# An MLP behind a spectral mixer: its products cut to 256 columns, the three terms summed in the same PSUM columns, Mish read from PSUM

## The chip, the core and the metric

The kernel runs on one core of one Trainium2 chip. The metric is the device time of one execution in microseconds, lower is better. A core has TensorE (PE; its weight loads are shown as PEld), VectorE (DVE), ScalarE (ACT), GpSimd (POOL) and SyncE (SP), each with its own instruction queue worked off in order, a scratch memory of 128 partitions (SBUF) and the accumulators that TensorE writes (PSUM, eight banks of 512 fp32 columns in each partition).

## The reference

For x of 2048 rows by 512, fp32:

```
mod = (silu(c) @ w_mod) -> sa, ca, ga, sb, cb, gb
h = layernorm(x) * (1 + ca) + sa
x = x + ga * irfft2(rfft2(h) * (w_r + i w_i))
h = layernorm(x) * (1 + cb) + sb
x = x + gb * (mish(h @ w1 + b1) @ w2)        # w1: 512 x 1376, w2: 1376 x 512
```

## The kernel before, in words

The first 130 us are the Fourier part, as products with constant matrices. Its end (`p3_col`, `p3_row`) runs over 16 groups of 128 rows; then comes the MLP, which the change touches.

**Precision.** Each MLP operand is split into a high part (a rounded fp32r copy, made by ScalarE) and a low part (the rest, made by VectorE). A product is three terms, high x high, high x low, low x high (`TERMS`); low x low is left out.

**Tiling.** The rows go in 8 blocks (`NB`) of 256 (two groups of 128). The 1376 hidden columns are 10 tiles of 128 and a narrow one of 96. A block has 6 steps (`NT`): step 0 has the narrow tile alone, steps 1 to 5 have two tiles each. In the last block step 0 comes last (`item`).

**First product, `up`.** For a tile of hidden columns the weights w1 (128 x 128 pieces, four along the 512 inputs) are the stationary operand, and the block's input h streams, its high and low part side by side as 2 x 256 columns. Four products with w1's high part stream all 512 columns into a bank: high x high in its columns 0 to 255, high x low in 256 to 511. Four with w1's low part stream the 256 high columns into 0 to 255. So the result lies in two halves that are still to be added.

**Activation, `front` and `back`.** Per tile ScalarE reads the right half of the bank and adds the bias b1 (L813), VectorE adds the left half (L814); then one Mish on ScalarE over both tiles, 512 columns in SBUF (L820), and four small sums and differences on VectorE (L830).

**Second product, `halves` and `down`.** `halves` splits the activations (`ah`, `al`, L765 and L766). `down` is done two steps after `up` (`LAG`). For a pair of hidden tiles and two groups of rows it uses a scheme with seven instead of eight block products (`RAW`, `SUM`, `END`), each 256 columns and three terms: 21 products a step (L856). Step 0 instead has 2 x 3 products of 512 columns with 96 rows of weights (L848). The last block does steps 3, 4, 5 and 0 in the plain way with 512 columns (`last_down`, L868 and L871).

**Next block's input.** In step 3 ScalarE normalises the next block's rows (`norm_pair`), in step 4 TensorE transposes them (`transpose_in`, L693, eight fp32 transposes), and ScalarE and VectorE scale, shift and split them (`split_in`, L701, L705, L706).

**Order.** The MLP is written out by hand: `mlp(s, parts)` gives each engine's queue its order. In step 4 TensorE has `up`, the transposes, then `down` of two steps ago. PSUM banks go by four tags A to D, two banks each, in rotation: A and D alternate for the two tiles of a step and serve the transposes; C, B, B, C are the four outputs of a block. The tile framework sets the waits between engines.

Of the kernel before, what the change touches and what calls it, by code (L numbers as in the profile page):

```python
# [9 lines left out]
AF = mybir.ActivationFunctionType  # L10
ALU = mybir.AluOpType

P = 128
S, D, F = 2048, 512, 1376
# [8 lines left out]
TERMS = ((0, 0), (0, 1), (1, 0))  # L23
# [3 lines left out]
LAG = 2  # L27
# [4 lines left out]
def tile_spectral_block(ctx: ExitStack, tc: tile.TileContext, x_d, w1_d, b1_d, w2_d,  # L32
                        c_d, xt_d, wm_d, wq_d, wz_d, kr_d, km_d, kc_d, ki_d, kf_d, kv_d, kw_d, kp_d, out_d):
    nc = tc.nc
# [33 lines left out]
    def bank(tag):  # L68
        return psum.tile([P, 512], F32, name="bank", tag=tag)

    def buf(tag, dt=F32):
        return work.tile([P, 512], dt, name="buf", tag=tag)

    def plain(t):
        return t.bitcast(F32)
# [6 lines left out]
    b1n = base.tile([P, NF], F32, name="b1n")  # L82
# [75 lines left out]
    def norm(n, late=False):  # L158
        h = buf("h")
        if late:  # L160
            nc.scalar.activation(h, x[:, n, :], AF.Identity, scale=rstd[:, n:n + 1], bias=nmr[:, n:n + 1])
            return h
        nc.gpsimd.tensor_scalar(h, x[:, n, :], rstd[:, n:n + 1], nmr[:, n:n + 1],
                                op0=ALU.mult, op1=ALU.add)
        return h

    st = {}
# [418 lines left out]
    with tc.manual_schedule():  # L586
# [13 lines left out]
        for p in range(pairs):  # L600
# [34 lines left out]
            if p in (3, 5):  # L635
                i = p // 2 - 1
# [9 lines left out]
    w1h = pm.tile([P, 4, NF * P], F32R, name="w1h")  # L646
    w1l = pm.tile([P, 4, NF * P], F32R, name="w1l")
    pm.tile([P, 16], F32, name="line")
    w2 = {}
# [24 lines left out]
    def h2_tiles(b):  # L674
        if b % 2 == 0:
            h2[b] = pm.tile([P, 4, 2, 256], F32R, name="h2e", tag="h2e")
        else:
            h2[b] = big.tile([P, 4, 2, 256], F32R, name="h2o", tag="cr")
# [4 lines left out]
    def norm_pair(n):  # L683
        st["h2", n] = norm(n, True), norm(n + 1, True)

    def transpose_in(n, g):
        if g == 0:
            h2_tiles(n // 2)
        st["pt2", g] = ps = bank("AD"[g] if n else "D")
        hs = st["h2", n]  # L690
        for k in range(2):
            for i, h in enumerate(hs):
                nc.tensor.transpose(ps[:, (2 * k + i) * P:(2 * k + i + 1) * P],  # L693
                                    h[:, (2 * g + k) * P:(2 * g + k + 1) * P], ident)

    def split_in(n, g):
        ps = st.pop(("pt2", g))
        t = buf("t")
        for e in reversed(range(2)):
            k = 2 * g + e  # L700
            nc.scalar.activation(t[:, 256 * e:256 * e + 256], ps[:, 256 * e:256 * e + 256],  # L701
                                 AF.Identity, bias=cols[:, 1, 0, k:k + 1], scale=cols[:, 1, 1, k:k + 1])
        tv = t.rearrange("p (k s) -> p k s", k=2)
        hh, hl = (h2[n // 2][:, 2 * g:2 * g + 2, i, :] for i in range(2))
        nc.scalar.copy(hh, tv)  # L705
        nc.vector.tensor_tensor(hl, tv, plain(hh), op=ALU.subtract)  # L706
# [36 lines left out]
    def item(g):  # L743
        b, i = divmod(g, NT)
        return b, (i + 1) % NT if b == NB - 1 else i

    def tiles(t):
        return [(0, NF - 1, F - (NF - 1) * P)] if t == 0 else [(e, 2 * t - 2 + e, P) for e in range(2)]
# [43 lines left out]
    ups, acts, out_ps, done = {}, {}, {}, {}  # L792
    tsum = modr[:, 0:2].rearrange("p r (e d) -> p (r e) d", d=256)

    def up(g):
        b, t = item(g)
        h = h2[b]
        ups[g] = []
        for e, f, rows in tiles(t):
            ps = bank("CD"[e] if g < 2 else "AD"[e])[:rows]  # L800
            fs = slice(f * P, f * P + rows)
            for k in range(4):
                nc.tensor.matmul(ps, w1h[:, k, fs], h[:, k], start=(k == 0), stop=False)  # L803
            for k in range(4):
                nc.tensor.matmul(ps[:, 0:256], w1l[:, k, fs], h[:, k, 0], start=False, stop=(k == 3))  # L805
            ups[g].append((e, f, ps))

    def front(g):
        st["w", g] = w = buf("g1")
        for e, f, ps in ups.pop(g):  # L810
            rows = ps.shape[0]
            o = w[:rows, 256 * e:256 * e + 256]
            nc.scalar.activation(o, ps[:, 256:], AF.Identity, bias=b1n[:rows, f:f + 1])  # L813
            nc.vector.tensor_tensor(o, o, ps[:, 0:256], op=ALU.add)  # L814

    def back(g):
        b, t = item(g)
        w = st.pop(("w", g))
        o = w if t else w[:96, 0:256]
        nc.scalar.activation(o, o, AF.Mish)  # L820
        if t == 0:
            return [(o, slice(0, 2))]
        if b == NB - 1 and t > 2:
            return [(w, slice(0, 4))]
        u = buf("g2")
        a = w.rearrange("p (e s) -> p e s", s=P)
        v = u.rearrange("p (e s) -> p e s", s=P)
        for o, p, q, op in ((v[:, 0], a[:, 0], a[:, 2], ALU.add), (v[:, 1], v[:, 0], a[:, 1], ALU.subtract),
                            (v[:, 2], a[:, 1], a[:, 0], ALU.subtract), (v[:, 3], a[:, 3], v[:, 1], ALU.subtract)):
            nc.vector.tensor_tensor(o, p, q, op=op)  # L830
        return [(w[:, P:], slice(0, 3)), (u, slice(3, 7))]

    def halves(g, parts):
        hi, lo = acts[g] = [act.tile([P, 7, P], F32R, name=n) for n in ("ah", "al")]
        for r, c in parts:
            split(*(z[:r.shape[0], c].rearrange("p e s -> p (e s)") for z in (hi, lo)), r)

    def down(g):
        b, t = item(g)
        if b == NB - 1 and t not in (1, 2):  # L840
            return last_down(g, t)
        a = acts.pop(g)
        out = out_ps.setdefault(b, None) or [bank(n) for n in "CBBC"]
        out_ps[b] = out
        if t == 0:
            for n, half in ((1, 1), (2, 0)):
                for i, (p, q) in enumerate(TERMS):
                    nc.tensor.matmul(out[n], a[p][:96, half], w2[0][q][:96], start=(i == 0), stop=False)  # L848
            return
        last = b == NB - 1  # L850
        end = t == (2 if last else 5)
        for n, half, e, r in END if last and end else RAW + SUM:
            o = out[n][:, 256 * half:256 * half + 256]
            own = last or n in (0, 3)
            for i, (p, q) in enumerate(TERMS):
                nc.tensor.matmul(o, a[p][:, e], w2[t][q][:, r], start=(own and half == 0 and t == 1 and i == 0),  # L856
                                 stop=(end and i == 2 and (n, half) != (1, 0)), skip_group_check=own)

    def last_down(g, t):
        a = acts.pop(g)  # L860
        if t == 3:
            out_ps["last"] = bank("A"), bank("D")
        for half in range(2):
            o = out_ps["last"][half]
            for f in range(2 if t else 1):
                for i, (p, q) in enumerate(TERMS):
                    if t:
                        nc.tensor.matmul(o, a[p][:, half + 2 * f], w2["plain", t][q][:, 512 * f:512 * f + 512],  # L868
                                         start=(t == 3 and f == 0 and i == 0), stop=False)
                    else:  # L870
                        nc.tensor.matmul(o, a[p][:96, half], w2[0][q][:96], start=False, stop=(i == 2))  # L871

    rows = modr[:, 0:2]

    def gather(b):
        out = out_ps[b]
        p, q = buf("h"), buf("h")
        nc.scalar.copy(p, out[0])
        nc.scalar.copy(q, out[3])
        done[b] = p, q  # L880
# [28 lines left out]
    def mlp(s, parts):  # L909
        b, i = divmod(s, NT)  # L910
        nxt = 2 * b + 2 if b < NB - 1 else None
        up(s)
        if i == 4 and nxt:
            for g in range(2):
                transpose_in(nxt, g)
        front(s)
        halves(s - 1, parts)
        parts = back(s)
        if i == 3 and nxt:
            norm_pair(nxt)  # L920
        if i == 4 and nxt:
            for g in range(2):
                split_in(nxt, g)
        down(s - LAG)
        if i == 1 and b:
            gather(b - 1)
            chain(b - 1)
        if i == 2 and b:
            residual(b - 1)
        if s == total - 3:  # L930
            gather(b)
            chain(b)
        if s == total - 2:
            residual(b)
        return parts
# [54 lines left out]
    h, l = (w.rearrange("p e d -> p (e d)")[:, 768:] for w in w2[3])  # L990
    nc.vector.tensor_tensor(l, tsum.rearrange("p e d -> p (e d)"), plain(h), op=ALU.subtract)
    halves(0, back(0))
    parts = back(1)
    load_w2(4)
    sum_w2(4, 0, 1, 2, 3)
# [164 lines left out]
```

## Time and profile before

| what | value |
|---|---|
| median of 3 runs | 379.59 us (379.28 to 380.18) |
| profiled execution | 379.18 us |
| its span, first to last instruction | 377.4 us |
| granted TensorE clock | 0.998 of full |
| busy: TensorE, weight loads, VectorE, ScalarE, GpSimd | 371.6, 332.9, 292.3, 240.0, 91.4 us |
| products and weight loads | 2809 each |
| the MLP's stretch | from 133.7 us to the end |

The page's busy time of TensorE is the union of overlapping products, so it says that one follows the other, not how fast they go. Rows of the chain of waits give a start, a length and a line with the count of instructions; rows of the timeline give start, length, engine, line, operation, output and inputs. In names, h2e and h2o are the inputs of even and odd blocks, w1h and w1l the parts of w1, w, w2hi, w2a, w2b, w2c the places of w2's parts, ah and al the activations' parts.

### The profile page before, as it was taken

Reading aid. Unit: us, or ns where it says so; the run is one execution under the profiler, and the core shown is the slowest. Engines: PE = TensorE matmul, PEld = TensorE weight load, DVE = VectorE, ACT = ScalarE, POOL = GpSimd, SP = SyncE. Lnnn points to the kernel's source line nnn. Section 1 sums busy time; section 2 is a strip of 40 time slices with the busy share of each in tenths; the row PEclk is TensorE's granted clock in tenths of the full one; section 3 lists DMA queues with packets and bytes.
Section 4 is the critical chain, followed back from the end, with each engine's and each line's share of the span. In section 5 each row is a group of like instructions: output and inputs, shape, how many; then the busy total and the mean of one; then the engine's idle time right before and its main releaser. Section 6 shows DMA issues by size and latency. Waiting matters only on the chain.

```text
span 377.4 us, 7443 instructions
## 1 busy us (share of the span) xinstructions
PE 371.6 (98%) x2809; PEld 332.9 (88%) x2809; DVE 292.3 (77%) x673; ACT 240.0 (64%) x535; POOL 91.4 (24%) x110
## 2 busy tenths in 40 slices
PE   8999999999999999999999999999999999999995
PEld 8899866668999988998999999998998999999984
DVE  1898989892878979879749758857966975988993
ACT  1688856855668447964945845855765674675650
POOL 0587725861974303300000000000000100026000
PEclk9999999999999999999999999999999999999999
DMA  7999998464332211000100100100100200221011
GB/s 241 376 337 344 326 378 320 141 197 131 104 103 73 81 30 56 2 0 8 50 2 1 57 0 2 56 2 1 58 2 0 76 2 0 85 75 67 3 56 56
DMA packets 20164, 36.78 MB, mean 97 GB/s; under 512 B 3713, under 2 KB 6625, under 8 KB 19873
## 3 DMA queue, kind: packets, MB, share of 16 engines
q1 hardware_dynamic: 20128, 36.31, 28.1%
q8 instruction: 22, 0.36, 0.4%
q14 instruction: 14, 0.11, 0.1%
HBM read 32.10 MB, written 4.20 MB: 96 GB/s over the span
## 4 chain that ended last, share of the span: by engine, by line
PE 94%; DVE 2%; ACT 2%; issue 1%; ACTq 0%
PE bank L856 24%; PE bank L803 21%; PE bank L805 10%; PE bank L531 4%; PE bank L504 4%; PE bank L724 4%; PE bank L715 4%; PE bank L714 4%; PE bank L211 3%; PE bank L256 3%; PE bank L848 3%; PE bank L868 2%; PE bank L693 2%; PE bank L267 1%; PE bank L479 1%; PE bank L257 1%
## 5 line engine op out<-in xcount | busy, mean ns | idle before, releaser
L813 ACT ACTIVATE buf<-bank,b1n 128x256 f32<-128x256 f32 (+1 forms) x88 | 40.8, 472 | 62.7 <-PE bank L805 59.9
L814 DVE TENSOR_TENSOR buf<-buf,bank 128x256 f32<-128x256 f32 (+1 forms) x88 | 35.3, 416 | 35.1 <-ACT buf L813 34.4
L766 DVE TENSOR_TENSOR al<-buf,ah 128x512 fp32r<-128x512 f32 (+2 forms) x85 | 53.7, 656 | 0.7 <-ACT ah L765 0.7
L803 PE MATMUL bank<-h2e,w1h 128*128 128x512 f32 (+1 forms) x176 | 47.9, 394 | 0.0
L803 PE MATMUL bank<-h2o,w1h 128*128 128x512 f32 (+1 forms) x176 | 47.8, 393 | 0.0
L785 POOL TENSOR_TENSOR buf<-buf,modr 128x512 f32<-128x512 f32 (+1 forms) x3 | 3.9, 1299 | 179.2 <-DVE buf L814 172.1
L765 ACT CAST ah<-buf 128x512 fp32r<-128x512 f32 (+2 forms) x85 | 43.0, 548 | 1.2 <-DVE buf L830 1.1
L830 DVE TENSOR_TENSOR buf<-buf 128x128 f32<-128x128 f32 x148 | 39.8, 310 | 3.5 <-ACT buf L820 2.2
L820 ACT ACTIVATE buf<-buf 128x512 f32<-128x512 f32 (+1 forms) x48 | 28.6, 597 | 15.9 <-DVE buf L814 15.8
L856 PE MATMUL bank<-w2a,ah 128*128 128x256 f32 x161 | 34.4, 283 | 0.0
L803 PEld LDWEIGHTS bank<-h2o,w1h 128*128 128x128 f32 (+1 forms) x176 | 29.8, 185 | 4.7 <-DVE buf L814 0.4
L803 PEld LDWEIGHTS bank<-h2e,w1h 128*128 128x128 f32 (+1 forms) x176 | 29.9, 186 | 4.3
L856 PE MATMUL bank<-w2b,ah 128*128 128x256 f32 x147 | 30.6, 277 | 0.0
L805 PEld LDWEIGHTS bank<-h2e,w1l 128*128 128x128 f32 (+1 forms) x176 | 26.5, 185 | 3.9
L805 PEld LDWEIGHTS bank<-h2o,w1l 128*128 128x128 f32 (+1 forms) x176 | 26.5, 185 | 3.9
L805 PE MATMUL bank<-h2e,w1l 128*128 128x256 f32 (+1 forms) x176 | 27.5, 278 | 0.0
L805 PE MATMUL bank<-h2o,w1l 128*128 128x256 f32 (+1 forms) x176 | 27.5, 278 | 0.0
L856 PEld LDWEIGHTS bank<-w2a,ah 128*128 128x128 f32 x161 | 26.3, 188 | 0.0
L715 PE MATMUL bank<-kc,d 128*128 128x128 f32 x128 | 24.8, 275 | 0.0
L714 PE MATMUL bank<-kc,d 128*128 128x128 f32 x128 | 24.7, 275 | 0.0
L856 PEld LDWEIGHTS bank<-w2b,ah 128*128 128x128 f32 x147 | 24.0, 188 | 0.0
L127 DVE BATCH_NORM_STATS2 st<-x 128x6 f32<-128x512 f32 x32 | 22.1, 689 | 0.6
(232 smaller groups left out, 944.8 us busy)
## 6 DMA issues: line engine op xcount, KB each, us to landing
buf<-in_B_w_dram SPq DMA_DIRECT2D x20, 256.0 KB, 2.6
x<-in_A_x_dram SPq DMA_DIRECT2D x16, 256.0 KB, 4.9
xring<-in_x_t_dram SPq DMA_DIRECT2D x16, 256.0 KB, 4.8
out_dram<-x SPq DMA_DIRECT2D x7, 512.0 KB, 2.6
mraw<-in_km_dram SPq DMA_DIRECT2D x16, 128.0 KB, 4.5
wqa<-in_w_q_dram SPq DMA_DIRECT2D x4, 512.0 KB, 6.0
early<-in_w_mod_dram SPq DMA_DIRECT2D x8, 256.0 KB, 6.5
wqb<-in_w_q_dram SPq DMA_DIRECT2D x4, 512.0 KB, 7.2
```

What stands on the lines that cost most here:

```text
L127: nc.vector.bn_stats(t, x[:, n, :])
L714: nc.tensor.matmul(o, dj[:, 0:128], kc[0][:, n, :], start=True, stop=False)
L715: nc.tensor.matmul(o, dj[:, 64:192], kc[1][:, n, :], start=False, stop=True)
L765: nc.scalar.copy(h, r)
L766: nc.vector.tensor_tensor(l, r, plain(h), op=ALU.subtract)
L803: nc.tensor.matmul(ps, w1h[:, k, fs], h[:, k], start=(k == 0), stop=False)
L805: nc.tensor.matmul(ps[:, 0:256], w1l[:, k, fs], h[:, k, 0], start=False, stop=(k == 3))
L813: nc.scalar.activation(o, ps[:, 256:], AF.Identity, bias=b1n[:rows, f:f + 1])
L814: nc.vector.tensor_tensor(o, o, ps[:, 0:256], op=ALU.add)
L820: nc.scalar.activation(o, o, AF.Mish)
L830: nc.vector.tensor_tensor(o, p, q, op=op)
L856: nc.tensor.matmul(o, a[p][:, e], w2[t][q][:, r], start=(own and half == 0 and t == 1 and i == 0), stop=(end and i == 2 and (n, half) != ( ...
```

## The change

All products of the MLP stream 256 columns. In `up` a tile's twelve products (four pieces of the inputs, three terms each) accumulate in the same 256 columns, the two tiles of a step in the two halves of one bank (tag A; C and D for the first two steps). `front` is then one Mish per tile, read from PSUM with the bias, and `back` keeps the four sums and differences. The 512-column products of step 0's `down` and of `last_down` become two of 256. In step 4 the transposes stand behind `down`, both in banks of tag D, as are the last block's two plain outputs. Where several groups share a bank, only its first product clears it.

```diff
 def transpose_in(n, g):
-        st["pt2", g] = ps = bank("AD"[g] if n else "D")
+        st["pt2", g] = ps = bank("D")
 def up(g):
+        ps = bank("CD"[g] if g < 2 else "A")
         for e, f, rows in tiles(t):
-            ps = bank("CD"[e] if g < 2 else "AD"[e])[:rows]
+            o = ps[:rows, 256 * e:256 * e + 256]
             fs = slice(f * P, f * P + rows)
             for k in range(4):
-                nc.tensor.matmul(ps, w1h[:, k, fs], h[:, k], start=(k == 0), stop=False)
-            for k in range(4):
-                nc.tensor.matmul(ps[:, 0:256], w1l[:, k, fs], h[:, k, 0], start=False, stop=(k == 3))
-            ups[g].append((e, f, ps))
+                for i, (p, q) in enumerate(TERMS):
+                    nc.tensor.matmul(o, (w1h, w1l)[p][:, k, fs], h[:, k, q], start=(e == 0 and k == 0 and i == 0),
+                                     stop=(e == len(tiles(t)) - 1 and k == 3 and i == 2), skip_group_check=True)
+            ups[g].append((e, f, o))
 def front(g):
-        for e, f, ps in ups.pop(g):
-            rows = ps.shape[0]
-            o = w[:rows, 256 * e:256 * e + 256]
-            nc.scalar.activation(o, ps[:, 256:], AF.Identity, bias=b1n[:rows, f:f + 1])
-            nc.vector.tensor_tensor(o, o, ps[:, 0:256], op=ALU.add)
+        for e, f, o in ups.pop(g):
+            rows = o.shape[0]
+            nc.scalar.activation(w[:rows, 256 * e:256 * e + 256], o, AF.Mish, bias=b1n[:rows, f:f + 1])
 def back(g):
-        o = w if t else w[:96, 0:256]
-        nc.scalar.activation(o, o, AF.Mish)
 def down(g):
         if t == 0:
             for n, half in ((1, 1), (2, 0)):
                 for i, (p, q) in enumerate(TERMS):
-                    nc.tensor.matmul(out[n], a[p][:96, half], w2[0][q][:96], start=(i == 0), stop=False)
+                    for c in range(0, D, 256):
+                        nc.tensor.matmul(out[n][:, c:c + 256], a[p][:96, half], w2[0][q][:96, c:c + 256],
+                                         start=(i == 0 and c == 0), stop=False, skip_group_check=True)
 def last_down(g, t):
-            out_ps["last"] = bank("A"), bank("D")
+            out_ps["last"] = bank("D"), bank("D")
...
+                    for c in range(0, D, 256):
...
 def mlp(s, parts):
         up(s)
-        if i == 4 and nxt:
-            for g in range(2):
-                transpose_in(nxt, g)
         front(s)
         halves(s - 1, parts)
         parts = back(s)
         if i == 3 and nxt:
             norm_pair(nxt)
+        down(s - LAG)
         if i == 4 and nxt:
             for g in range(2):
+                transpose_in(nxt, g)
+            for g in range(2):
                 split_in(nxt, g)
-        down(s - LAG)
```

**TensorE, step 4 of a block.** The end of `up`, the transposes and the start of `down`; before:

```order
L803 MATMUL bank<-h2e,w1h 128x512 x4
L805 MATMUL bank<-h2e,w1l 128x256 x4
L693 MATMUL bank<-ident,buf 128x128 x8
L856 MATMUL bank<-w2a,ah 128x256 x2
L856 MATMUL bank<-w2a,al 128x256
```

and now:

```order
L805 MATMUL bank<-h2e,w1h 128x256 x2
L805 MATMUL bank<-h2e,w1l 128x256
L855 MATMUL bank<-w2a,ah 128x256 x2
L855 MATMUL bank<-w2a,al 128x256
L693 MATMUL bank<-ident,buf 128x128 x8
L805 MATMUL bank<-h2e,w1h 128x256 x2
```

The second product of two steps ago now stands ahead of the transposes, and the next step's first product directly behind them; within a tile the weights alternate high, high, low.

**ScalarE, start of the MLP** (L131 and L132 are the last group's normalisation, the next rows the first two steps' activations), as a difference:

```order
 L132 ACTIVATE bank<-bank 128x4 [waits Activation_49]
+L813 ACT_TABLE_LOAD
 L813 ACTIVATE buf<-bank,b1n 96x256 [waits PE_49]
-L813 ACTIVATE buf<-bank,b1n 128x256 [waits PE_49] x2
-L820 ACT_TABLE_LOAD
-L820 ACTIVATE buf<-buf 96x256 [waits DVE_49]
+L813 ACTIVATE buf<-bank,b1n 128x256 [waits PE_49]
+L813 ACTIVATE buf<-bank,b1n 128x256
 L765 CAST ah<-buf 96x256 [waits Activation_49]
```

The table of functions is loaded ahead of the first tile, the wait on VectorE's sum is gone, and the two tiles of a step have one wait on TensorE in place of two.

More of the change, by code (lines that the diff above doesn't have):

```diff
@@ L818, in back @@
         w = st.pop(("w", g))
-        o = w if t else w[:96, 0:256]
-        nc.scalar.activation(o, o, AF.Mish)
         if t == 0:
-            return [(o, slice(0, 2))]
+            return [(w[:96, 0:256], slice(0, 2))]
         if b == NB - 1 and t > 2:
@@ L856, in down @@
                 nc.tensor.matmul(o, a[p][:, e], w2[t][q][:, r], start=(own and half == 0 and t == 1 and i == 0),
-                                 stop=(end and i == 2 and (n, half) != (1, 0)), skip_group_check=own)
+                                 stop=(end and i == 2 and (n, half) != (1, 0)), skip_group_check=True)
     def last_down(g, t):
@@ L866, in last_down @@
                 for i, (p, q) in enumerate(TERMS):
[L867 to L871, printed above, removed]
+                    for c in range(0, D, 256):
+                        if t:
+                            l, r = a[p][:, half + 2 * f], w2["plain", t][q][:, 512 * f + c:512 * f + c + 256]
+                        else:
+                            l, r = a[p][:96, half], w2[0][q][:96, c:c + 256]
+                        nc.tensor.matmul(o[:, c:c + 256], l, r, start=(t == 3 and f == 0 and i == 0 and c == 0),
+                                         stop=(t == 0 and i == 2 and c > 0), skip_group_check=True)
     rows = modr[:, 0:2]
```

## The prediction

> **What bounds the kernel now.** I read the page's engine shares first.
>
> ```profile
> PE 371.6 (98%) x2809; PEld 332.9 (88%) x2809; DVE 292.3 (77%) x673; ACT 240.0 (64%) x535; POOL 91.4 (24%) x110
> ```
>
> TensorE sets the end. A busy PE may still be waiting inside a group, so the second view is the chain of waits over one block of six steps, merged by line. Column two is the time from a group's start to the next group's start.
>
> ```profile
> 211.11 0.87 PE bank L693 x8
> 211.98 2.47 PE bank L856 x21
> ...
> 219.71 0.92 PE bank L803 x4
> 220.64 0.47 PE bank L805 x4
> 221.10 2.38 PE bank L856 x21
> 223.48 0.91 PE bank L803 x4
> 224.40 0.47 PE bank L805 x4
> 224.87 0.93 PE bank L803 x4
> 225.80 0.45 PE bank L805 x4
> 226.25 2.38 PE bank L856 x21
> ...
> 230.94 0.45 PE bank L805 x4
> 231.40 1.39 PE bank L848 x6
> ...
> 240.80 0.87 PE bank L693 x8
> ...
> 330.75 2.48 PE bank L856 x21
> ```
>
> One group follows another without a hole, from the transposes at 211.11 to the next at 240.80. So the time is the number of products times their pitch. There are two pitches for the same product of 256 columns: 2.47/21 = 117.6 ns and 2.38/21 = 113.3 ns, held over all 21. Four products of 512 take 0.91 or 0.93, 230 ns each on average, which is two of 115. **Fast stretches** stand only after the narrow tile (the 96 hidden columns, 219.71) and after a tile whose four short products took 0.45. **Slow stretches** follow the transposes, at 211.98 as behind the seventh and last (330.75). Between, the four 512-column products of a tile turn the pitch over: the tile at 223.48 comes out of a fast stretch and ends slow (0.47), the next ends fast again (0.45).
>
> The third view, what the weight loads waited for from 134 us on, has four rows in all, these the longest:
>
> ```profile
> PEld bank L848 <- DVE al L766: 0.5, 1, 0.5
> PEld bank L803 <- DVE buf L814: 0.4, 1, 0.4
> ```
>
> One is where the MLP starts, the other in its last 13 us. The steady part has no wait to remove.
>
> **The change, part by part.**
>
> *Work taken from ScalarE and VectorE.* Per full step two Identity reads of PSUM, two adds and one Mish become two Mish reads of PSUM.
>
> ```profile
> L813 ACT ACTIVATE buf<-bank,b1n 128x256 f32<-128x256 f32 (+1 forms) x88 | 40.8, 472 | 62.7 <-PE bank L805 59.9
> L814 DVE TENSOR_TENSOR buf<-buf,bank 128x256 f32<-128x256 f32 (+1 forms) x88 | 35.3, 416 | 35.1 <-ACT buf L813 34.4
> L820 ACT ACTIVATE buf<-buf 128x512 f32<-128x512 f32 (+1 forms) x48 | 28.6, 597 | 15.9 <-DVE buf L814 15.8
> ```
>
> A Mish from PSUM isn't in the trace; I price it as the Identity of that form, 472 ns (Mish over 512 columns at 597 and two Identities at 472 bound it from 0.3 to 0.6 us). VectorE loses 35.3 us, ScalarE 28.6 us, and all of it lies beside TensorE: worth 0 in the steady part. The first Mish now waits for both tiles of its step, 1.4 us later than the first Identity; its products are used two steps on, so that costs 0.
>
> *The stalls go.* At the start the chain runs through ScalarE:
>
> ```profile
> 138.26 1.22 ACT L813 ACTIVATE buf<-bank,b1n 96x256 f32<-96x256 f32 x3
> 139.50 1.28 ACT L820 ACT_TABLE_LOAD   x1
> 141.24 0.41 ACT L765 CAST ah<-buf 96x256 fp32r<-96x256 f32 x1
> 141.68 0.78 DVE L766 TENSOR_TENSOR al<-buf,ah 96x256 fp32r<-96x256 f32 x1 [0.36 <-ACT ah L765]
> 141.70 0.50 PE L848 MATMUL bank<-w2b,ah 96*128 96x512 f32 x1
> 364.98 1.15 PE bank L803 x4
> 366.60 5.65 PE bank L868 x24
> ```
>
> The first L848 lost 0.5 there to the low half (the wait above). With the table load first, then three Mish (1.22), the cast starts at 138.3 + 1.28 + 1.22 = 140.8 and the low half is ready at 141.6 to 142.0; it is first read four short products after 141.6, at 142.07. I take 0.5 as saved, and 0.2 as the low end. At the end 1.15 against 0.93 is 0.22, and 5.65/24 = 235 against 230 is 0.11: VectorE's adds that made those two late are gone. Sum: **-0.8 us**.
>
> *512 columns become twice 256.* 88 tiles gain 4 products each, the halves of step 0 gain 42, the last block's products 42: 436 more products and weight loads, same columns. In units of 256 the MLP has 88 x 12 + 37 x 21 + 84 + 84 = 2001. Now: the block from 211.98 to 240.80 is 28.82 us for 249 units, 115.8 each, 231.7 us for all. After, no 512 is left to turn the pitch, and every unit is at 113.3 or at 117.6: 226.7 us or 235.3 us, -5.0 or +3.6. Those are the two ends; which units run at which pitch decides. My reading: the transposes set slow, the narrow tile sets fast, all else keeps what it finds. Then slow are: step 0 to the first transposes, 162 units; behind each of the first six transposes 24 + 21 and half a narrow tile, 51, so 306; behind the seventh 279, as no narrow tile comes before the end. Total 747 at 117.6 and 1254 at 113.3: 229.9 us, **-1.8 us**.
>
> [...]
>
> *The fifth step's transposes behind its second product.* The eight transposes (0.87, the change of operand type included) are as many as before, and no DMA moves. They now stand behind the 21 products of L856, before the next step's tiles. On ScalarE everything behind the read of the transposes queues:
>
> ```profile
> 241.21 1.02 ACT L765 CAST ah<-buf 128x384 fp32r<-128x384 f32 x2
> 242.67 1.01 ACT L701 ACTIVATE buf<-bank,cols 128x256 f32<-128x256 f32 x2
> 245.28 0.62 ACT L705 CAST h2e<-buf 128x512 fp32r<-128x512 f32 x1
> 245.94 0.69 DVE L706 TENSOR_TENSOR h2e<-buf,h2e 128x512 fp32r<-128x512 f32 x1 [0.88 <-ACT h2e L705]
> 243.99 1.08 PE L803 MATMUL bank<-h2o,w1h 128*128 128x512 f32 x4
> 246.77 0.28 PE L856 MATMUL bank<-w2hi,ah 128*128 128x256 f32 x1
> 249.24 1.09 PE L803 MATMUL bank<-h2e,w1h 128*96 128x512 f32 x4
> 250.63 0.39 PE L856 MATMUL bank<-w2b,ah 128*128 128x256 f32 x2
> ```
>
> Both reads and casts took 242.67 to 245.90, 3.2 us. In these times they would now start near 244.1 and end at 247.4; VectorE's low half (0.69) makes the new block's input ready near 248.1, needed at 249.24. The next step's Mish (0.9), ready to run at 246.9, is held to 247.4, its casts (1.0) and the last subtraction end near 249.9, needed at 250.63. Margins 1.1 and 0.7 us; 57 products between them at the fast pitch take 0.25 away. I cost the part at 0; if ScalarE's queue ran 1.2 us later than worked out here, TensorE would wait 0.5 us a block, 7 x 0.5 = +3.5 us.
>
> **The sum**: -0.8 - 1.8 + 0 = -2.6. The profiled execution took 379.18 us (span 377.4 and 1.8 around it), the median of three is 379.59, 0.1% more; from the median, **377.0 us**.
>
> **The rivals.**
>
> *A: fast nearly throughout, 373.8 us* (-5.0 - 0.8). The fast stretches last as long as nothing disturbs them, at exactly one pitch, so a slow stream may fall into it by itself. Against: no slow stretch of 21 did. Chance 0.18.
>
> *B: nothing sets fast; slower, 382.4 us* (+3.6 - 0.8). One mechanism: the transposes put TensorE on 117.6, and only the 512s had taken it off. It decides at the narrow tile of each block. For: the very last narrow tile, entered after a wait, took 0.47 for its four short products, no sign of fast. Against: in six blocks 2.38 follows directly on it. Chance 0.22.
>
> ```profile
> 366.12 0.47 PE bank L805 x4
> ```
>
> *C: no change that can be told, 378.8 to 380.0 us.* The change of 128 to 96 rows in L848 sets slow too: its six 512s (231.40) take 232 each although the tile ahead ended fast (230.94). Then only 96 units in each of six blocks are fast, 1425 x 117.6 + 576 x 113.3 = 232.8, +1.1, and with -0.8 the end is at 379.9. So does a fixed price of 2 ns on each extra product, within what the rows allow (2 x 113.3 - 230 = -3, 2 x 117.6 - 230 = +5): 436 x 2 = +0.9, 379.7. With the pitches mixed as now the end is 378.8. [...] Chance 0.20.
>
> **How the numbers follow.** Forecast 0.40, A 0.18, C 0.20, B 0.22. What a measurement can tell from no change is 0.2%, 0.8 us. The forecast and A are faster, and a quarter of C: 0.63. Three quarters of C, less a little that reaches beyond: 0.13. B and that rest: 0.24. The forecast's own range is 375.4 to 378.4 (fast stretches longer or shorter by 250 units, 1.1 us, and the stalls' 0.4). The range to record reaches past A, over C and into the near side of B, where some stretches are fast: 373.5 to 381.9; what lies above is the fully slow half of B and a late split, about 0.15.
>
> **What would show it.** In the chain of waits: x21 groups at 2.38 behind each narrow tile and on to the next transposes, at 2.47 behind the transposes only; a tile of 24 at 2.72 or 2.82, nothing between. B: 2.47 everywhere. C: 2.47 behind L846 (the halves). The waits above should be gone; a wait of TensorE on the new block's input or on a high half, once a block, would show the moved transposes too late. VectorE's busy time should fall to about 257 us and ScalarE's to about 211 with no effect of their own. The prediction is wrong if the pitch changes inside a group, or if a third pitch appears.

## The result, and the profile after

The changed kernel takes 376.96 us (median, 376.28 to 377.35) against 379.43 us before: a ratio on record of 0.9924, 95% interval 0.9907 to 0.9941 (the two medians alone give 0.9935). In a later series it took 377.75 us against 379.94, 0.9938 (0.9920 to 0.9957). It is faster by 0.6 to 0.8%, and the predicted 377.0 us lies between. Much of the spread between the profiled executions lies ahead of the MLP: its first product starts anywhere from 133.5 to 135.7 us, behind stages that no kernel here touches. The sharper measure is therefore the MLP's own stretch, from the start of its first product to the start of the last add in the chain of waits: 239.06 us before, 236.43 us after.

The page of the changed kernel, engine shares and the two groups whose work changed:

```profile
PE 368.0 (98%) x3245; PEld 349.6 (93%) x3245; DVE 261.6 (70%) x585; ACT 213.9 (57%) x487; POOL 91.3 (24%) x110
...
L813 ACT ACTIVATE buf<-bank,b1n 128x256 f32<-128x256 f32 (+1 forms) x88 | 37.3, 471 | 90.8 <-PE bank L805 76.7
L827 DVE TENSOR_TENSOR buf<-buf 128x128 f32<-128x128 f32 x148 | 42.5, 328 | 1.3
```

TensorE is still at 98%. Mish from PSUM takes 471 ns. VectorE and ScalarE have lost 30.7 and 26.1 us of work, which was on the path only at the start of the MLP (see the transposes at their old place, below). L827, the four sums that stood at L830, became slower, 310 to 328 ns each.

The chain of waits of the changed kernel (start, length, group), at the MLP's start, over a block's boundary, and at its end:

```profile
133.46 1.37 PE bank L805 x12
...
135.72 5.66 PE bank L805 x48
...
153.40 0.87 PE bank L693 x8
154.27 2.83 PE bank L805 x24
...
159.57 1.37 PE bank L805 x12
160.94 2.38 PE bank L855 x21
163.32 2.72 PE bank L805 x24
...
229.78 1.37 PE bank L846 x12
231.15 2.73 PE bank L805 x24
...
333.02 2.47 PE bank L855 x21
...
369.89 1.37 DVE x L944 x2
```

There is no third pitch. A tile of 24 takes 2.83 or 2.72 us (118 or 113 ns a product), a group of 21 2.47 or 2.38. Behind the transposes (153.40) both are slow, the narrow tile (159.57) turns the pitch, and from there on all is fast to the next transposes, through step 0's twelve products at 229.78 as well. The last block, with no narrow tile until its end, is slow. Inside a group the pitch changes only in the narrow tile, as the sum had it. The view of waits lists none of TensorE or of its weight loads in the MLP any more; in the kernel before it lists four.

A slow stretch and the fast one behind it, as windows (start and end, length, busy time of TensorE, weight loads, VectorE, ScalarE and GpSimd, then the granted clock, the DMA engines' busy share and GB/s):

```profile
153.40:159.60 6.20, 6.20 (x55) 6.20 (x54) 4.76 (x10) 5.65 (x12) 1.43 (x2) 1.00 0.00 0
159.60:182.70 23.10, 23.10 (x206) 23.10 (x205) 15.94 (x37) 11.47 (x24) 0.00 (x0) 1.00 0.06 24
```

The granted clock is 1.00 in both, and the DMA engines are idle in the slow one, so neither the clock nor transfers make the difference.

### The profile page after: what moved, and what is told of

The parts are those of the page before. It is cut to its first block, busy times and chain, and to the rows that moved or that the text cites. A ratio compares the mean times of both kernels' runs of the same rounds, so it can differ in the third digit from the quotient of the medians.

```text
span 374.3 us, 8202 instructions
## 1 busy us (share of the span) xinstructions
PE 368.0 (98%) x3245; PEld 349.6 (93%) x3245; DVE 261.6 (70%) x585; ACT 213.9 (57%) x487; POOL 91.3 (24%) x110
## 4 chain that ended last, share of the span: by engine, by line
PE 94%; DVE 2%; DMA 1%; ACT 1%; issue 1%; SPq 0%; ACTq 0%
PE bank L805 32%; PE bank L855 24%; PE bank L531 4%; PE bank L504 4%; PE bank L715 4%; PE bank L714 4%; PE bank L724 4%; PE bank L211 3%; PE bank L256 3%; PE bank L846 3%; PE bank L871 2%; PE bank L693 2%; PE bank L479 1%; DMA wmc<-in_w_mod_dram 1%; PE bank L257 1%; PE bank L258 1%
## 5 line engine op out<-in xcount | busy, mean ns | idle before, releaser
L805 PE MATMUL bank<-h2e,w1h 128*128 128x256 f32 (+1 forms) x352 | 62.3, 279 | 0.0
L805 PE MATMUL bank<-h2o,w1h 128*128 128x256 f32 (+1 forms) x352 | 62.1, 278 | 0.0
L805 PEld LDWEIGHTS bank<-h2e,w1h 128*128 128x128 f32 (+1 forms) x352 | 52.8, 185 | 0.0
L805 PEld LDWEIGHTS bank<-h2o,w1h 128*128 128x128 f32 (+1 forms) x352 | 52.8, 185 | 0.0
L805 PE MATMUL bank<-h2e,w1l 128*128 128x256 f32 (+1 forms) x176 | 48.8, 277 | 0.0
L805 PE MATMUL bank<-h2o,w1l 128*128 128x256 f32 (+1 forms) x176 | 48.8, 277 | 0.0
L827 DVE TENSOR_TENSOR buf<-buf 128x128 f32<-128x128 f32 x148 | 42.5, 328 | 1.3
L805 PEld LDWEIGHTS bank<-h2e,w1l 128*128 128x128 f32 (+1 forms) x176 | 32.6, 185 | 0.0
L805 PEld LDWEIGHTS bank<-h2o,w1l 128*128 128x128 f32 (+1 forms) x176 | 32.6, 185 | 0.0
L855 PEld LDWEIGHTS bank<-w2a,ah 128*128 128x128 f32 x161 | 26.1, 188 | 0.0
L701 ACT ACTIVATE buf<-bank,cols 128x256 f32<-128x256 f32 x32 | 16.3, 560 | 8.9 <-PE bank L693 8.9
L256 PE MATMUL bank<-buf,mring 128*128 128x512 f32 x48 | 20.7, 430 | 0.3 <-DVE buf L249 0.2
```

The source lines that it names most:

```text
L256: nc.tensor.matmul(pa, m[:, a, 0:128], g, start=(i == 0), stop=False)
L805: nc.tensor.matmul(o, (w1h, w1l)[p][:, k, fs], h[:, k, q], start=(e == 0 and k == 0 and i == 0), stop=(e == len(tiles(t)) - 1 and k == 3 a ...
```

## The experiments

The table has the profiled execution's MLP stretch, worked out from two rows of the chain of waits as above, and the products counted at each pitch by their starts in the trace (fast up to 115 ns, slow 116 to 119; 23 to 38 products of each kernel take longer, most of them 120 to 123 ns, and are in neither). Where an expectation gives the MLP's length "to its last product", it is 0.6 us more than the stretch given here.

| kernel | stretch, us | slow | fast | time, us | ratio to before (interval) |
|---|---|---|---|---|---|
| before | 239.06 | 512s mixed in | | | |
| changed | 236.43 | 694 | 1280 | 376.96 | 0.9924 (0.9907 to 0.9941) |
| changed, again | 236.52 | 704 | 1264 | 377.75 | 0.9938 (0.9920 to 0.9957) |
| the cut alone | 237.46 | 820 | 1152 | 378.69 | 0.9960 (0.9946 to 0.9975) |
| changed, step 0's six left at 512 | 239.04 | 1216 | 664 | 379.67 | 0.9995 (0.9980 to 1.0010) |
| changed, transposes at the old place | 236.98 | 825 | 1152 | 377.80 | 0.9954 (0.9939 to 0.9970) |
| input early | 235.93 | 494 | 1470 | 377.62 | 0.9947 (0.9928 to 0.9966) |
| narrow tile later at the start | 236.00 | 557 | 1415 | 376.66 | 0.9920 (0.9899 to 0.9941) |
| both | 235.34 | 361 | 1601 | 377.09 | 0.9923 (0.9906 to 0.9940) |
| both, two waits removed | 233.61 | 65 | 1905 | 374.59 | 0.9851 (0.9826 to 0.9876) |

**The cut alone.** The kernel before, with its 512-column products as two of 256 each; halves of the bank, VectorE's add, Mish and the transposes stay.

```diff
-                nc.tensor.matmul(ps, w1h[:, k, fs], h[:, k], start=(k == 0), stop=False)
+                for q in range(2):
+                    nc.tensor.matmul(ps[:, 256 * q:256 * q + 256], w1h[:, k, fs], h[:, k, q],
+                                     start=(k == 0 and q == 0), stop=False, skip_group_check=True)
...
```

> The kernel before with nothing but its 512-column products cut into pairs of 256 (left and right half of the bank, VectorE's add, the separate Mish and the place of the transposes stay). Theory (the pitch of a product is a state that transposes set slow, the narrow tile sets fast, and 512-column products turn over): 1.1 to 1.4 us faster than before, near 378.2, with slow stretches of 21 + 24 + 21 units behind each transposes, fast ones from the third product of each narrow tile, and the waits at the MLP's start and end still there. Rival 1 (the gain came from the work taken off ScalarE and VectorE): no change, 379.4. Rival 2 (a 512-column product is simply dearer than two of 256, the same everywhere): the full steady gain, 2 to 2.5 us, near 377.

The stretch fell by 1.60 us, the time by 1.4. The cut alone brings more than half of the gain, and most of that by the pitch, as its chain of waits shows:

```profile
143.51 0.65 PE bank L852 x4
...
154.41 2.48 PE bank L861 x21
...
162.19 0.92 PE bank L804 x8
...
163.56 2.38 PE bank L861 x21
```

The group behind the transposes is slow, the one behind the narrow tile (162.19) fast. At 143.51 four products take 0.65 us where 0.47 would do: the start's stall is still there. By the products' starts it costs 0.48 us beyond the pitch, where it cost 0.58 before. The waits in the last 13 us, which I expected to stay, are gone, though VectorE's adds are not: TensorE, slow through the whole last block, comes to the narrow tile when they are done (365.4 against 365.3 us). They had cost 0.36 us. So 0.46 of the 1.60 us are waits, and 1.14 are pitch, the low end of what I expected.

**Step 0's six products left at 512 columns**, all else as changed.

> The changed kernel with only the six products of step 0's second product (the halves, 96 rows) put back to 512 columns: 42 of the 436 cuts undone. Theory: the stretch behind them, up to the next transposes, goes at one pitch throughout. If six wide products leave the pitch slow, 90 units in each of six blocks go from 113.3 to 117.7, +2.4 us, near 379.3, and the gain is gone; if they leave it fast, within 0.3 us of the changed kernel. Rival 1: no change, 377.0. Rival 2 (a fixed price per product): a tenth of the gain is lost, +0.2 us, and all 256-column products elsewhere keep their pitch.

42 products in the whole kernel, six a block, left uncut take the whole gain away: the stretch is 2.6 us longer. The chain of waits of this kernel:

```profile
169.05 2.72 PE bank L805 x24
171.77 1.39 PE bank L845 x6
173.16 2.83 PE bank L805 x24
175.99 2.47 PE bank L854 x21
```

The six themselves cost 1.39, as the twelve halves cost 1.37. What they cost is behind them: everything up to the next narrow tile is slow.

**The transposes at their old place**, ahead of step 4's second product, all else as changed.

> The changed kernel with the transposes back in their old place, ahead of the second product of step 4. Theory: the 21 products behind them turn slow in blocks 1 to 6, 6 x 21 x 4.4 ns = +0.55 us, near 377.5; ScalarE reads the transposes earlier and TensorE waits for nothing either way. Rivals 1 and 2: no change, 377.0; if the late transposes held ScalarE up and cost something, this kernel is faster.

```profile
181.10 0.87 PE bank L693 x8
181.97 2.47 PE bank L855 x21
184.44 2.83 PE bank L805 x24
```

Now 21 more products a block stand between the transposes and the narrow tile, 126 in six blocks (825 slow against 694 to 704), and the stretch is 0.5 us longer. That is all the moved transposes are worth, and it is what 126 products lose between the two paces (126 x 4.4 ns = 0.55 us).

Beside the cut alone, whose transposes stand at the same place, this kernel also shows what the work taken from VectorE and ScalarE and the new order of a tile's products are worth. From the first transposes to the seventh both take 176.48 us by the products' starts: nothing. Ahead of the first it is 18.02 us for the cut alone and 17.54 here: the stall of the start, and the whole difference between the two.

**Extra products behind the transposes.** Two runs of the changed kernel, each with a few more products of 256 columns (four of 512 in one place) behind each block's transposes, whose result nobody reads; their number and the width of their weights differ from block to block.

```diff
...
+    PROBES = ((96, 256, 3), (128, 256, 3), (96, 256, 1), (64, 256, 3), (128, 512, 4), (96, 256, 2), (96, 256, 3))
...
+    PROBES = ((96, 3), (96, 3), (96, 3), (96, 6), (64, 12), (96, 4), (96, 6))
...
```

> The changed kernel with a few extra products behind the transposes of each block, whose result nothing reads: block 0 three of 96 weight columns, block 1 three of 128, block 2 one of 96, block 3 three of 64, block 4 four of 128 with 512 streamed columns, block 5 two of 96, block 6 three of 96. About 2.6 us of extra products. Theory: behind three narrow ones (blocks 0, 3, 6) the next 24 products go at 113.3 and stay there; behind three of full width (block 1) at 117.7; behind four of 512 fast or slow, not between; one or two narrow ones decide nothing known, the narrow tile turned at its third product. In block 6 the whole last block is then fast, about 230 units, -1.0 us. Rival 3 (it isn't the narrow weights that turn the pitch but the new block's input or a step's boundary): 117.7 behind all of them, up to the next narrow tile.

> The changed kernel with extra products of 256 columns, whose result nobody reads, behind each block's transposes: 3, 3 and 3 of 96 weight columns in blocks 0, 1 and 2, 6 of 96 in block 3, 12 of 64 in block 4, 4 of 96 in block 5, 6 of 96 in block 6. Asked of each: are the 24 and 21 products behind it at 113.3 (2.72 and 2.38) or at 117.7 ns (2.83 and 2.47)? Theory 1 (enough products with narrow weights turn it, three are on the edge): blocks 3, 5 and 6 fast, 0 to 2 mixed, and the last block fast to its end, -1.2 us there against 0.5 to 0.9 us for each block's extra products; block 4 fast too, if 64 columns do as 96. Theory 2 (what turned in block 0 before was that place in the stream, not the number): block 0 fast, 1 and 2 slow and block 6 slow again. Theory 3 (64 columns never turn it, as a group of 64 takes its own pitch): block 4 slow with twelve. The time is about that of the changed kernel plus 3 us for the probes and less what they turn, 378 to 380.

The first run took 378.61 us, the second 380.19 (single runs). What followed the probes, from the chains of waits and the products' starts:

| weight columns, count | behind it |
|---|---|
| 96, three | fast in 2 places, slow in 3 |
| 96, four; 96, six (twice) | fast |
| 96, one or two | slow |
| 64, three; 64, twelve | slow |
| 128, three | slow |
| 128, four of 512 columns | fast |

Three places of the second run's chain of waits: three and six probes of 96 columns and twelve of 64, each with the tile behind it.

```profile
213.61 0.35 PE bank L916 x3
213.96 2.83 PE bank L805 x24
...
243.27 0.69 PE bank L916 x6
243.96 2.72 PE bank L805 x24
...
273.07 1.41 PE bank L916 x12
274.48 2.83 PE bank L805 x24
```

So a block boundary or a new input is not what turns the pitch; products with 96 weight columns are, if there are enough of them (four were, three were on the edge), and in the one place tried four products of 512 columns were too. 64 columns were not, though narrower, in one place with three and one with twelve. In the first run I expected the last block to be fast behind three probes of 96, and it was not; with six, in the second, it was, from 333.4 to 352 us. Then one wait of 0.6 to 0.8 us came, on an output bank that VectorE was still reading, and it was slow again: that a wait resets the pitch was in none of the theories.

**The narrow tile later at the start.** Step 1's first tile stands in its place as cover between the last two groups of the Fourier part, and the narrow tile follows the last of these.

```diff
...
         if s == 15:
-            up(0)
+            up(1, slice(0, 1))
         if s == 16:
-            up(1)
+            up(0)
+            up(1, slice(1, 2))
```

> The changed kernel, with the first tile of step 1 in place of the narrow tile as cover between the last two groups of the inverse transform's products; the narrow tile follows behind the last of these, then the second tile of step 1. Same instructions. My theory (the slow stretch at the start of the MLP is set by those fp32 products, the narrow tile takes it off): 12 slow units, then the narrow tile and 126 units at 113.3 up to the first transposes, 138 x 4.4 ns = -0.6 us against the changed kernel (about 376.4 where that stands at 377.0); the first groups of 21 at 2.38. Rival (the first steps are slow for a reason of their own, such as the first reading of each weight): 2.47 there still, no gain. If the narrow tile's halves come late, which now have 4.1 us of products ahead of them in place of 5.7, TensorE waits ahead of the halves of step 0 and the gain is eaten: a wait of 0.5 us leaves nothing.

```profile
135.66 1.42 PE bank L807 x12
...
137.97 5.45 PE bank L807 x48
...
147.51 2.38 PE bank L857 x21
```

The 48 products behind L724 take 5.45 us in place of 5.66, now with the narrow tile at their head, and the first groups of 21 are at 2.38: the slow start was set by L724's fp32 products. 137 slow products fewer, 0.43 us off the stretch where 0.6 was expected; in the time itself it can't be told from the changed kernel.

**A block's input early**, its transposes one block forward, straight ahead of a narrow tile.

```diff
-        nxt = 2 * b + 2 if b < NB - 1 else None
+        nxt = 2 * b + 4 if b < NB - 2 else None
...
+        if i == 5 and nxt:
+            for g in range(2):
+                transpose_in(nxt, g)
+            split_in(nxt, 0)
+        if i == 0 and 0 < b < NB - 1:
+            split_in(2 * b + 2, 1)
```

> The changed kernel, with the transposes of a block's input moved one block forward: those for block b+2 stand at the end of the sixth step of block b, straight ahead of the narrow tile of block b+1; only block 1's stay in the fifth step of block 0. Same products, same transposes, same reads. My theory (transposes set 117.7 ns, the narrow tile sets 113.3 at its third product, all else keeps what it finds): slow are the 150 units ahead of the first transposes, 47 behind them, and 2 or 3 behind each of the other six, some 210 in place of about 710, so 500 x 4.4 ns = 2.2 us less than the changed kernel, about 374.8 where that stands at 377.0; the last block is at 2.38 for 21 and 2.72 for 24 to its end. Rival 1 (the narrow tile turns the pitch only because products of 128 columns stand between it and the transposes, as three narrow products failed once straight behind them): slow from the first such transposes on, 1.4 us x 3.5 more than the changed kernel, about 382. Rival 2 (the last block is slow by its own weights, not by what precedes it): only the six stretches of 47 less, of which one is block 0's and stays, 5 x 45 x 4.4 ns = -1.0 us, 376.0, with the last block at 2.47 and 2.83.

**Both reorderings in one.**

> Both reorderings in one: a block's input transposed straight ahead of a narrow tile, and the narrow tile behind the inverse transform's last products at the start. My theory: the two gains add, -2.2 and -0.6, so 374.2 where the changed kernel stands at 377.0 (1.4% under the kernel before); slow are about 70 units of 2001, and the MLP's products take 2001 x 113.3 = 226.7 us and 0.3. If rival 1 of the early input holds, about 381.5; if rival 2, 375.4; if the start's order brings a wait, it is no better than the early input alone.

Both missed: 0.5 and 1.1 us off the stretch where 2.2 and 2.8 were expected, and in the time neither can be told from the changed kernel (0.9947 and 0.9923 against 0.9924 and 0.9938). In these two some 0.4 us of the gain is lost outside the span from first to last instruction: their profiled executions take 2.4 us more than that span, the others 1.8 to 2.0; why is open. The narrow tile does turn the pitch straight behind the transposes (rival 1 falls), but 494 products were slow, not 210, and 361 in the kernel with both, not 70. Where the fast pitch was lost, in the kernel with both (the early input alone loses it in the same two places), by its chain of waits and what its weight loads waited for:

```profile
165.06 2.72 PE bank L807 x24
167.78 2.70 PE bank L857 x21
170.47 2.83 PE bank L807 x24
...
192.89 2.38 PE bank L857 x21
...
349.17 2.56 PE bank L857 x21
351.73 2.83 PE bank L807 x24
```

```profile
PEld bank L857 <- DVE w2b L766: 0.2, 1, 0.2
```

A group at 167.78 takes 2.70 because the low half of step 5's weight sums came 0.2 us late (the new input's reads stood ahead of it on ScalarE), and everything is slow from there to the next narrow tile, ahead of 192.89. At 349.17 the group takes 2.56: one product was held back by 16 ns at an output bank that VectorE was still reading (129 ns between two starts in place of 113, and 222 to the next), and the 106 products behind it are slow.

**Both, with the two waits removed.** The input's reads move to where VectorE and ScalarE have time, and in the last block's second step the chain that frees the banks goes ahead of the four sums.

```diff
-        parts = back(s)
+        late = i == 1 and b == NB - 1
+        if not late:
+            parts = back(s)
...
-            split_in(nxt, 0)
-        if i == 0 and 0 < b < NB - 1:
-            split_in(2 * b + 2, 1)
+        if i in (2, 3) and 0 < b < NB - 1:
+            split_in(2 * b + 2, i - 2)
...
             chain(b - 1)
+        if late:
+            parts = back(s)
```

> Both reorderings of the run before, with the two waits out of the way that stood in its trace: the new input's reads of PSUM move from the sixth step and the first to the third and fourth step of the next block (they had made the low half of the sums of the sixth step's weights late, 0.2 us at 168 us), and in the last block's second step the sums of the activations stand behind the chain that frees the output banks (TensorE had waited a few ns for them at 349.6 us). Theory as it now stands (any wait of TensorE sets 117.7 ns, however short, as the transposes do; the narrow tile sets 113.3): with no wait some 62 units of 2001 are slow in place of 361, so 299 x 4.4 ns = 1.3 us and the waits' own 0.35 less: first product to last of the MLP 234.3 us in place of 235.95 (the changed kernel: 237.0), the time 2.7 under the changed kernel, about 374.2 where that stands at 377.0. Rival (block 1 and the last block are slow by a property of their own there, such as the first use of the sixth step's weights, or the last block's plain weights): 2.47 and 2.83 stay in both places though nothing waits, 236 us.

> The changed kernel once more, beside the run above on the same chip: 376.5 to 377.5 by its runs so far; the first product to the last of its MLP 237.0 us again, whatever the stages ahead of it take.

```profile
133.85 1.42 PE bank L807 x12
...
169.11 2.72 PE bank L807 x24
...
352.12 2.38 PE bank L857 x21
...
357.22 2.72 PE bank L873 x24
...
367.46 1.37 DVE x L957 x2
```

Fast in both places, and to the end: 65 slow products, a stretch of 233.61 us where 234.3 less 0.6 was expected, and 374.59 us. This version beats both kernels, the one before by 1.5% and the changed one by 0.8%, with the same products, transposes and reads. The changed kernel again, beside it on the same chip, took 377.75 us, a little above what I expected, with its stretch at 236.52. So the last block's pitch is no property of its weights, and the waits were what had taken the early input's gain.

**One wait, made on purpose.** The changed kernel, with one more product behind the up-projection of step 3 of blocks 1 to 6; in blocks 1 to 3 its operand comes late from GpSimd.

```diff
...
+        v = h2[b][:, 0, 0]
+        if b < 4:
+            w = st["w", s]
+            v = buf("y", F32R)[:, 0:256]
+            nc.gpsimd.tensor_tensor(v, w[:, 0:256], w[:, 256:], op=ALU.add)
+        nc.tensor.matmul(bank("A")[:, 0:256], w1h[:, 0, 0:P], v, start=True, stop=True)
...
```

> The changed kernel with one more product of 256 columns and 128 weight columns, whose result nobody reads, behind the up-projection of the fourth step of blocks 1 to 6. In blocks 1, 2 and 3 its moving operand is the sum, made by GpSimd, of the two halves of that step's Mish, which is not there for 1 us or more, so TensorE stands still; in blocks 4, 5 and 6 it is the block's input, which is there. Asked: the pitch of the 21, 24 and 21 products between it and the next transposes, in a stretch that is at 113.3 ns in the changed kernel. Theory (a wait sets the slow pitch): 2.47, 2.83, 2.47 behind it in blocks 1 to 3; 2.38, 2.72, 2.38 in blocks 4 to 6. Rival (only a product of another type, or work that stands in the same stretch, sets it): 2.38, 2.72, 2.38 in all six. Time about 3 x 1.3 us above the changed kernel, and 3 x 0.3 more by the theory.

What TensorE waited for (us in all, times, longest), then its chain behind the first wait, behind the second, and at block 5's extra product (which had no wait), then a window behind the second wait, with the granted clock in the column after POOL's busy time:

```profile
PE bank L916 <- POOL buf L915: 5.8, 3, 1.9
```

```profile
178.94 2.48 PE bank L855 x21
181.42 2.83 PE bank L805 x24
...
210.87 4.00 PE bank L855 x21
...
220.17 0.87 PE bank L693 x8
221.05 2.73 PE bank L805 x24
...
304.67 0.11 PE bank L916
304.79 2.38 PE bank L855 x21
```

```profile
210.40:214.80 4.40, 4.32 (x23) 4.32 (x24) 3.08 (x7) 1.37 (x2) 0.03 (x1) 0.61 0.29 119
```

The first wait leaves the slow pitch behind it, the products without a wait leave the fast one: as the theory has it. The second and the third do more. Behind each of them, 15 products run at 213 ns, with the granted clock at 0.61 over the window shown. The third also left nine products at 113 ns ahead of that, so a wait does not always set slow; and the transposes at 220.17, behind the second, are followed by the fast pitch. The single run took 388.93 us, some 6 us above what I expected: the waits were 2 us each, not 1, and half the clock cost another 3.0 (30 products at 213 ns in place of 113).

## Why the prediction was right

**What bounds the kernel** (the number of products times their pitch, two pitches, which groups set them) held in the changed kernel. I forecast 747 slow and 1254 fast units; 694 and 1280 were counted, among other things because the narrow tile turned after two products and not after six. Over the changed kernel and the runs made since, the transposes, with no extra product or narrow tile behind them, left the slow pitch in 51 of 52 places. In every block behind the first the narrow tile was fast by its eighth product at the latest, in the changed kernel from its third on in blocks 1 to 6. At the start of the MLP it turned in 10 of 12 traces; in the changed kernel's second trace and in the one with waits made on purpose, all twelve of its products there were slow. So the reading holds nearly always, but not always.

**The sum of -2.6** came out at -2.63 on the stretch (239.06 to 236.43). By whole stretches its terms look shared out differently:

| term | predicted | measured, by stretches |
|---|---|---|
| 512 to 2 x 256, the transposes' place apart | part of -1.8 | 239.06 - 237.46 = -1.60 |
| moved transposes | 0 as work; their pitch is in the -1.8 | 236.98 - 236.43 = -0.55 |
| stalls, with the work taken off two engines | -0.8 | 236.98 - 237.46 = -0.48 |

By these rows cut and place make -2.15 where I had -1.8, and the stalls -0.48 where I had -0.8. But the first row holds 0.46 us of waits, as shown above. With these put to the stalls, the pitch brought -1.69 (-1.14 and -0.55) and the stalls -0.94: both terms are within 0.15 of the forecast, which therefore did not come out by misses that cancel. (28.82 us over 249 units are 115.7 ns, not the 115.8 of the prediction; this makes its own pitch term -1.7.) The reason I gave for the 0.33 at the end, that VectorE's adds are gone, was not needed: the cut alone keeps the adds and loses those waits.

The 0 for the moved transposes was right as to their cover (no wait came), but the step that costs them says nothing of the 21 products they free from the slow pitch; these were counted in another step, where the reader could not see their worth.

**Mish from PSUM**: 471 ns for the 472 I took. **VectorE and ScalarE**: 261.6 and 213.9 us for some 257 and 211; the four sums became slower, 2.7 us in all, which I had not thought of. As forecast, none of it was worth anything in the steady part (176.48 us with it and without it).

**Rival A** (fast throughout by itself) fell: in the changed kernel the stream never went over to the fast pitch without a narrow tile. Its 373.8 us is near what the last version reaches, where order, not chance, makes the stream fast. **Rival B** (nothing sets fast) fell at 159.57. **Rival C** (step 0's products set slow) fell at 231.15; its observation was sound, since the same products at 512 columns do set slow, which the run with six of them showed. Its other branch, a price per product, fell too: 436 more products made the stretch 1.6 us shorter, 1.1 of it by the pitch, with nothing else changed. The Trainium skill, "TensorE: Matmul & The Clock Gate", section "Back-to-back issue gap", gives a single product some 2.5 ns beside its columns. At that price 436 more would have cost +1.1 us, an estimate from that page; the trace does not agree with it here.

**What the reading lacked** is the last half sentence, "all else keeps what it finds". It held in the changed kernel only because nothing there waits in a fast stretch. In the kernels built on it, a product held back by 16 ns was followed by 106 slow ones, and the same reading failed by 1.7 us twice.

## What to carry to other kernels

When one engine is the bound and never waits, compare equal groups along its chain before costing anything: two lengths for the same work mean that something ahead of the group sets its pace, and the order of the work is then worth as much as its amount. Here the changed kernel's own instructions in another order, with no wait left in it, gained another 2.8 us of stretch. And price a short wait on such an engine by what runs behind it, not by its own length.

## What the runs showed of the hardware

- A stream of products of 256 fp32r columns with 128-column weights has two paces, 113.3 and 117.7 ns each, and keeps either for hundreds of products. fp32 transposes or other fp32 products, six 512-column products with 96-row operands, and seven of the eight waits that came in a fast stretch, one that held a product back by 16 ns included, left the slow one. Four or more products with 96 weight columns left the fast one, except for the twelve at the start of the MLP in two of twelve traces. Four products of 512 columns left it behind the transposes in one place; in the kernel before, four of them left either (the 0.47 and the 0.45 behind them, at 224.40 and 225.80 in the rows of the prediction). 64 weight columns did not, twelve in a row. The granted clock was 1.00 at both paces. Why 96 columns turn it and 64 do not, and why three of 96 did in two places and not in three, stays open: no run here shows what the two paces are made of.
- A stand of TensorE of 2 us cost, in two of three places, half the clock for 15 products (213 ns each; granted clock 0.61 over 4.4 us behind the second wait). The Trainium skill, "TensorE: Matmul & The Clock Gate", section "HAM oscillation — how this bites in real kernels", puts the danger at gaps of more than about 3.4 us; here 2 us, with a dense stream before and behind, was enough, so the measurement decides.
- The first fp32r product behind the transposes starts the second one 199 to 205 ns later in place of 118, some 84 ns each time; behind a wait, with no change of type, it was 222 to 229.
